# Sink-window attention before two expert layers: folding two pairs' scores in one copy, and moving the attention output ahead of the second pair's maxima

## The chip, the cores and the metric

The program runs on one core of a Trainium2 chip. The metric is the device time of one execution in microseconds (us). The kernel before was run three times: 624.0, 624.75 and 624.91 us, median 624.75. The execution that was profiled took 624.49 us, of which 622.70 are the span that the profiler shows; 1.79 us lie around it.

## What is computed

Inputs are float32: 2 batches, 8 heads, 768 positions, head dimension 64.

```python
scores = scale * np.matmul(q, k.transpose(0, 1, 3, 2))
keep = is_sink | in_window        # pos < 4, or 0 <= rel < 128
scores = np.where(keep, scores, -1000000000.0)
a = np.exp(scores - np.max(scores, axis=-1, keepdims=True))
a = a / (np.sum(a, axis=-1, keepdims=True) + 1e-09)
x = np.matmul(a, v)               # -> 1536 tokens x 512
h = x @ w_in1                     # 512 -> 2048, rational function P(h)/Q(h)
x = g(h) @ w_out1
h = np.maximum(x @ w_in2, 0.0)    # second layer: squared relu
out = (h * h) @ w_out2
```

The expert weights arrive as 64-bit numbers, so each weight tile has to be loaded and narrowed on the chip before TensorE can use it.

## The kernel before, in words

**Two parts.** The first part is the attention, written as steps. A step `u` is one block of 128 query positions with all 8 heads; there are 12 (`NU`), 6 for each batch. The second part is the two expert layers, written as 96 "slots" `k` (48 for each layer). A slot computes one 128-wide slice of the hidden layer for 512 tokens: `g1` (12 matmuls of 512 columns, L620), an elementwise chain on ACT, DVE and POOL (`act_a`, `act_b`, `act_c`), and `g2` (12 matmuls, L699). The last steps of the attention are interleaved with the first slots: `slot(0)` runs `step(12)` in its middle, `slot(1)` runs `step(13)`. The order of instructions on every engine is the order in which the Python program writes them; each engine works its queue strictly in that order.

**One attention step.** Heads come in four pairs `pr`; a half `a` of a step holds two pairs (`k` = 0, 1), and the two heads of a pair are `e` = 0, 1. In step `u` the engines do this, for work of several steps at once:

- TensorE: `scores(u, 0)` and `scores(u, 1)` (L363) multiply the queries with 272 key columns: the block to the left (128 keys and 8 sink columns) and the block's own (128 keys). Only 264 columns are written, and the second pair starts at column 248 (`OFF`) of the same bank. Then `sinks_t(u-2)` (L422) and `trans(u-1)` (L429) transpose earlier results, `pv(u-2)` (L465) multiplies probabilities with values into the one bank called `O`, and `sinks_and_sums(u-2)` (L480, L484) adds the sink keys' values and spreads the reciprocal sums.
- DVE: `fold(u, a)` first copies scores under a mask. A query at place t in its block sees its own block's key j where t >= j, and the left block's key j where t < j, so the two blocks share 128 columns. The copy (`copy_predicated`, L375) is one instruction for a pair, 128 x 2 x 128. Then one custom instruction for each head (L384) adds the mask, scales, writes the negated scores to a tile `ns` (six buffers), and gives their minimum (`nmax`, the negated maximum). `result(u-3)` (L490) multiplies bank `O` with the reciprocals `rb` into `xf`. `sums(u-1)` (L417, L418) adds eps and inverts the sums. At a step's end come steps of the weight narrowing (`w_until`, L241, L247, L253), three to a tile.
- ACT: `expo` (L401) turns `ns` into probabilities and their sums, `trans` copies transposes out (L433), `sinks` and `sinks_t` copy sink columns (L410, L424), `sinks_and_sums` copies `rb` (L486), and `w_fin` rounds a narrowed weight tile (L274).
- POOL: `w_fin` subtracts the rounded weight from the exact one (L275), `parts_of(u-3)` rounds `xf` into `xh` (L497) and takes the remainder `xl` (L498), and `halves(u-1)` splits probabilities into left and own block (L445, L449; L443 in a batch's first block).

**Banks.** PSUM has two score tiles of two banks each (tag `S`), two banks `T`, one `U` and one `O`. `ps_t(tail=True)` takes a bank of a score tile in place of another; the last steps use it. The expert layers' sums (`g2`) also take the two score tiles. With a single bank `O`, the values of step u can be written only after `result(u-1)` has read it:

```python
def pv(m):
    u, a = divmod(m, 2)
    if a == 0:
        ops[u] = ps_t("O")
```

The masks `m_1` and `m_2` for a batch's second block and for later blocks are made once by `setup_rest`, partly on ACT (L140, L147), during steps 0 and 1.

The functions that the change touches, with the line numbers of the profile:

Of the kernel before, what the change touches and what calls it, by code (L numbers as in the profile page):

```python
# [28 lines left out]
NA = 7  # L29
# [9 lines left out]
def kernel(  # L39
# [13 lines left out]
    nc = tc.nc  # L53
# [4 lines left out]
    NU = B * NB  # L58
# [79 lines left out]
    def setup_rest(rel, win, snk, tmp, m_1, m_2, tri):  # L138
        def addm_s(dst, src):
            nc.scalar.activation(out=dst, in_=src, func=ACTF.Identity, scale=BIG, bias=nbig)  # L140

        nc.vector.tensor_scalar(out=tri, in0=rel[:, P:], scalar1=0.0, scalar2=None, op0=ALU.is_lt)
        nc.gpsimd.tensor_tensor(out=tmp, in0=win[:, 0:P], in1=win[:, P:], op=ALU.add)
        nc.gpsimd.tensor_tensor(out=win[:, P:P + SK], in0=snk[:, 0:SK], in1=win[:, 0:SK], op=ALU.subtract)
        yield
        addm_s(m_1[:, SK:], tmp)
        nc.scalar.activation(out=win[:, P:P + SK], in_=win[:, P:P + SK], func=ACTF.Relu)  # L147
        addm_s(m_1[:, 0:SK], win[:, P:P + SK])
        yield
        addm_s(m_2[:, SK:], tmp)  # L150
        addm_s(m_2[:, 0:SK], snk[:, 0:SK])

    def setup_moe():
        nc.scalar.mul(out=na, in_=ab[:, 0:4], mul=-1.0)
# [111 lines left out]
    def w_fin():  # L266
        m = wst["fin"]
        if m not in wx or len(spare) <= keep[0] or int(spare[0][1:]) >= len(wpool):
            return
        wst["fin"] += 1  # L270
        xf = wx.pop(m).bitcast(F32)
        tag = spare.pop(0)
        t = wpool[int(tag[1:])].tile([P, 2, DM], F32R, tag=tag, name="w")
        nc.scalar.copy(out=t[:, 0], in_=xf)  # L274
        nc.gpsimd.tensor_tensor(out=t[:, 1], in0=xf, in1=t[:, 0].bitcast(F32), op=ALU.subtract)  # L275
        W[wtiles[m]] = (t[:, 0], t[:, 1], tag)

# [16 lines left out]
    def attention(ap, extra):  # L294
# [51 lines left out]
        def scores(u, a):  # L346
            i = u % NB
            t = ss[a]
            for k in (1, 0):
                pr, o = 2 * a + k, OFF * k  # L350
                d = [t[:, e, o:] for e in range(2)]
                if i == 0:
                    for e in range(2):
                        s = slice(D * e, D * e + D)
                        nc.tensor.matmul(
                            d[e][:, 0:P], lhsT=ld[u, "q"][s, pr, :], rhs=keys[s, pr, 0, 0:P], start=True, stop=True
                        )
                else:
                    hf = P // 2
                    for g in range(2):  # L360
                        for e in range(2):
                            s, r = slice(D * e, D * e + D), slice(hf * g, hf * g + BS + hf)
                            nc.tensor.matmul(  # L363
                                d[e][hf * g:hf * g + hf, r], lhsT=ld[u, "q"][s, pr, hf * g:hf * g + hf],
                                rhs=keys[s, pr, i - 1:i + 1, :].rearrange("p i n -> p (i n)")[:, r],
                                start=True, stop=True,
                            )

        def fold(u, a):
            i = u % NB  # L370
            mask, co, bw = (m_0, 0, P) if i == 0 else (m_1 if i == 1 else m_2, P, BS)
            pairs = [(k, ss[a][:, :, OFF * k:]) for k in (1, 0)]
            for _, t in pairs:
                if i:
                    nc.vector.copy_predicated(  # L375
                        out=t[:, :, BS:BS + P], mask=tri.unsqueeze(1).to_broadcast([P, 2, P]), data=t[:, :, 0:P]
                    )
            for k, t in pairs:
                n = u * NPR + 2 * a + k
                ns = []  # L380
                for e in range(2):
                    ix = 2 * n + e
                    x = ap.tile([P, 160], F32, name="ns", bufs=6)
                    nc.vector.tensor_tensor_reduce(  # L384
                        out=x[:, 0:bw], in0=t[:, e, co:co + bw], in1=mask, scale=-scale, scalar=3.0e38,
                        op0=ALU.add, op1=ALU.min, accum_out=nmax[:, ix:ix + 1],
                    )
                    ns.append(x)
                kps[n] = ns

        def expo(n):
            u, pr = divmod(n, NPR)
            w = BS if u % NB else P
            if u not in pe_t:
                pe_t[u] = ap.tile([P, NPR, 2, ROW], F32, name="pe", bufs=2)
                rs_t[u] = ap.tile([P, 32], F32, name="rs", bufs=3)[:, 0:H]
            rs, t = rs_t[u], pe_t[u][:, pr]
            ns = kps.pop(n)
            for e in range(2):
                ix = u * H + 2 * pr + e  # L400
                nc.scalar.activation(  # L401
                    out=t[:, e, ROW - w:], in_=ns[e][:, 0:w], func=ACTF.Exp, scale=-1.0,
                    bias=nmax[:, ix:ix + 1], accum_out=rs[:, 2 * pr + e:2 * pr + e + 1],
                )
            pr_t[n] = t

        def sinks(u):
            t = pe_t.pop(u)
            if u % NB:
                nc.scalar.copy(  # L410
                    sr[u % 2][:, 0:HS].rearrange("p (r e s) -> p r e s", r=NPR, e=2),
                    t[:, :, :, ROW - BS:ROW - P],
                )

        def sums(u):
# [10 lines left out]
        def trans(m):  # L426
            d = ps_t(tail=m >= NM - 2)
            for j in range(4):
                nc.tensor.transpose(  # L429
                    d[:, j * P:(j + 1) * P], pr_t[2 * m + j // 2][:, j % 2, ROW - P:], ident  # L430
                )
# [23 lines left out]
        def pv(m):  # L455
            u, a = divmod(m, 2)
            if a == 0:
                ops[u] = ps_t("O")
            pt = pT.pop(m)
            for r in range(2):  # L460
                pr = 2 * a + r
                for j in range(2):
                    for e in range(2):
                        if pt[j] is not None:
                            nc.tensor.matmul(  # L465
                                ops[u][D * e:D * e + D, pr * P:(pr + 1) * P],
                                lhsT=ld[u - 1 + j, "v"][:, 2 * pr + e, :], rhs=pt[j][:, 2 * r + e],
                                start=(pr == 0 and (j == 0 or pt[0] is None)),
                                stop=(pr == NPR - 1 and j == 1), skip_group_check=True,
                            )  # L470
# [58 lines left out]
        def step(u):  # L529
# [6 lines left out]
                        fill(ps_t("T"), DENSE[u][a])  # L536
            if u < NU and u and u % NB == 0:
                sink_keys(u)
            if u < NU:
                fold(u, 0)  # L540
            if 0 <= u - 3:
                result(u - 3)
                parts_of(u - 3)
            if u == 0:
                sink_keys(0)
                rest = setup_rest(*next(masks), m_1, m_2, tri)
                next(rest)
                next(rest)
            if 0 <= u - 1 < NU:
                sinks(u - 1)  # L550
                sums(u - 1)
            if 0 <= u - 2 < NU:
                sinks_t(u - 2)
            if u < NU:
                expo(u * NPR + 1)
            if 0 <= u - 1 < NU:
                trans(2 * u - 2)
                trans(2 * u - 1)
            if u < NU:
                expo(u * NPR)  # L560
                fold(u, 1)
            if u == 1:
                next(rest, None)
            if 0 <= u - 2 < NU:
                pv(2 * u - 4)
# [1 line left out]
            if 0 <= u - 1 < NU:  # L567
                halves(2 * u - 2)
                halves(2 * u - 1)
            if u < NU:  # L570
                expo(u * NPR + 3)
            if 0 <= u - 2 < NU:
                sinks_and_sums(u - 2)
            if u < NU:
                expo(u * NPR + 2)
            if u == 0:
                for t in sr:
                    nc.gpsimd.memset(t, 0.0)
# [6 lines left out]
                load(u + 1, "v")  # L585
            if u < NU and u % NB == 0:
                load_sinks(u // NB)
            if u >= 3:
                for _ in range(4):
                    next(moe, None)  # L590
            if u == NU - 1:
                g1(0)
            if u < NU and u % NB == 1:
# [459 lines left out]
    with tc.tile_pool(name="ap", bufs=1) as ap:  # L1053
        NM = NU * NPR // 2

        def extra(u):
            for _ in range((1, 1, 2)[u] if u < 3 else 0):
                w_load()
            w_until(min(WS * NA, 2 * u))
            if u == NU:  # L1060
                conv["on"] = False
            if u == NU + 1:
                conv["tag"], conv["on"] = "O", True

        attention(ap, extra)
# [49 lines left out]
```

## Time and profile before

| what | value |
|---|---|
| median of 3 runs | 624.75 us (624.0 to 624.91) |
| the profiled execution | 624.49 us, span 622.70 us |
| TensorE busy with matmuls | 599.8 us, 96% of the span |
| DVE, ACT, POOL busy | 428.5, 347.6, 338.6 us |
| share of the chain of waits that ends last | PE 81%, DVE 10%, ACT 6% |
| attention alone (steps 0 to 11) | up to about 78 us |
| last interleaved steps (slots 0 and 1) | about 78 to 98 us |

How to read it: PE is TensorE's matmuls, PEld its weight loads, PEclk the clock that TensorE was granted (1.00 is 2.4 GHz, 0.50 is 1.2 GHz). Busy time of an engine is summed over the whole span, and the two parts of this kernel have different limits, so rows of one stretch say more than the totals. The trace prints a line that holds an instruction and what it waited for; times in it start at the beginning of the span.

### The profile page before, as it was taken

The numbers are of one execution on the slowest core, as the hardware profiler recorded it, in microseconds if no ns is written. First come the engines' busy times: TensorE is split into PE (matmuls) and PEld (weight loads), VectorE is DVE, ScalarE is ACT, GpSimd is POOL, SyncE is SP. The second block draws the span as 40 slices with busy tenths as digits, with TensorE's granted clock in tenths as the row PEclk, the third lists the DMA queues.
The fourth block names the chain that finished last, engine by engine and source line by source line (L and its number), as shares of the span: only waits on it lengthen the run. The fifth ranks groups of instructions, "written<-read, shape, count | busy, mean of one in ns | idle before, by whom it ended". The sixth has DMA issues, their size and how long they took to land.

```text
span 622.7 us, 9780 instructions
## 1 busy us (share of the span) xinstructions
PE 599.8 (96%) x3490; PEld 492.4 (79%) x3490; DVE 428.5 (69%) x875; ACT 347.6 (56%) x734; POOL 338.6 (54%) x309
## 2 busy tenths in 40 slices
PE   7798889999999999999999999999999999999995
PEld 5676778788888878888888888888888888888884
DVE  5998836989989899877768879598594422441421
ACT  5988855888886877877869543243332222222210
POOL 4688765777776767666857575444352222222221
PEclk9999998999999999999999999999999999999999
DMA  8965311422332333111111447557466355500102
GB/s 212 284 184 170 107 35 35 129 83 93 103 103 75 98 98 102 36 67 34 35 34 35 114 157 251 188 175 235 132 207 198 111 194 169 179 25 0 68 0 73
DMA packets 64233, 72.05 MB, mean 116 GB/s; under 512 B 15281, under 2 KB 55217, under 8 KB 64177
## 3 DMA queue, kind: packets, MB, share of 16 engines
q1 hardware_dynamic: 64032, 71.35, 37.3%
q8 instruction: 29, 0.48, 0.3%
q14 instruction: 28, 0.22, 0.1%
q10 hardware_dynamic: 144, 0.00, 0.0%
HBM read 68.20 MB, written 3.15 MB: 115 GB/s over the span
## 4 chain that ended last, share of the span: by engine, by line
PE 81%; DVE 10%; ACT 6%; issue 1%; POOL 0%; DVEq 0%; ACTq 0%
PE s L699 37%; PE T L620 30%; PE U L620 7%; PE O L465 3%; ACT pe L401 2%; PE O L480 1%; DVE ns L384 1%; DVE t L674 1%; DVE U L672 1%; DVE t L670 1%; DVE wx L253 1%; PE s L511 1%; DVE xf L490 1%; ACT U L666 1%; DVE part L728 1%
## 5 line engine op out<-in xcount | busy, mean ns | idle before, releaser
L620 PE MATMUL T<-xh,w 128*128 128x512 f32 x640 | 210.9, 391 | 0.7 <-DVE t L649 0.7
L682 POOL TENSOR_TENSOR gl<-g,gh 128x512 fp32r<-128x512 f32 x48 | 62.2, 1295 | 157.9 <-ACT gh L681 157.8
L620 PEld LDWEIGHTS T<-xh,w 128*128 128x128 f32 x640 | 120.1, 188 | 28.1 <-DVE t L649 2.8
L699 PE MATMUL s<-gh,w 128*128 128x512 f32 x384 | 126.0, 389 | 0.0
L620 PE MATMUL T<-xl,w 128*128 128x512 f32 x320 | 124.6, 389 | 0.0
L699 PE MATMUL s<-w,gh 128*128 128x512 f32 x384 | 118.2, 389 | 0.0
L682 POOL TENSOR_TENSOR gl<-t,gh 128x512 fp32r<-128x512 f32 x48 | 62.2, 1296 | 47.2 <-ACT gh L681 46.3
L275 POOL TENSOR_TENSOR w<-wx,w 128x512 fp32r<-128x512 f32 x64 | 82.8, 1294 | 7.9 <-ACT w L274 7.7
L699 PEld LDWEIGHTS s<-w,gh 128*128 128x128 f32 x384 | 72.1, 188 | 15.1
L699 PEld LDWEIGHTS s<-gh,w 128*128 128x128 f32 x384 | 72.1, 188 | 14.9
L641 POOL TENSOR_TENSOR t<-t,ah 128x512 f32<-128x512 f32 x48 | 62.2, 1297 | 36.6 <-ACT t L638 34.7
L681 ACT CAST gh<-g 128x512 fp32r<-128x512 f32 x48 | 29.9, 623 | 82.1 <-PE s L699 74.8
L699 PE MATMUL s<-gl,w 128*128 128x512 f32 x192 | 74.7, 389 | 0.0
L699 PE MATMUL s<-w,gl 128*128 128x512 f32 x192 | 74.7, 389 | 0.0
L620 PEld LDWEIGHTS T<-xl,w 128*128 128x128 f32 x320 | 60.1, 188 | 12.3
L681 ACT CAST gh<-t 128x512 fp32r<-128x512 f32 x48 | 29.9, 622 | 45.8 <-DVE t L674 40.1
L670 DVE SCALAR_TENSOR_TENSOR t<-t,U 128x512 f32<-128x512 f32 x48 | 33.0, 686 | 30.3 <-ACT U L667 30.2
L655 DVE TENSOR_TENSOR g<-r,T 128x512 f32<-128x512 f32 x32 | 21.8, 683 | 42.5 <-ACT r L645 42.5
L645 ACT ACTIVATE r<-T 128x512 f32<-128x512 f32 x32 | 19.2, 600 | 53.2 <-PE T L620 53.1
L274 ACT CAST w<-wx 128x512 fp32r<-128x512 f32 x64 | 39.3, 616 | 6.4 <-DVE wx L253 6.4
L620 PE MATMUL U<-xh,w 128*128 128x512 f32 x128 | 42.1, 390 | 0.0
L699 PEld LDWEIGHTS s<-gl,w 128*128 128x128 f32 x192 | 36.0, 188 | 7.6
(136 smaller groups left out, 1016.4 us busy)
## 6 DMA issues: line engine op xcount, KB each, us to landing
wr<-in_w_in_dram SPq DMA_DIRECT2D x54, 512.0 KB, 4.1
wr<-in_w_out_dram SPq DMA_DIRECT2D x52, 512.0 KB, 3.8
qr<-in_q_dram SPq DMA_DIRECT2D x12, 256.0 KB, 4.7
keys<-in_k_dram SPq DMA_DIRECT2D x12, 256.0 KB, 4.7
vr<-in_v_dram SPq DMA_DIRECT2D x12, 256.0 KB, 5.2
wr<-in_v_dram SPq DMA_DIRECT2D x6, 512.0 KB, 4.5
out_dram<-part SPq DMA_DIRECT2D x12, 256.0 KB, 2.0
vsc<-in_v_dram SPq DMA_DIRECT2D x2, 16.0 KB
```

The costliest lines, as they stand in the source:

```text
L274: nc.scalar.copy(out=t[:, 0], in_=xf)
L275: nc.gpsimd.tensor_tensor(out=t[:, 1], in0=xf, in1=t[:, 0].bitcast(F32), op=ALU.subtract)
L401: nc.scalar.activation(out=t[:, e, ROW - w:], in_=ns[e][:, 0:w], func=ACTF.Exp, scale=-1.0, bias=nmax[:, ix:ix + 1], accum_out=rs[:, 2 * p ...
L465: nc.tensor.matmul(ops[u][D * e:D * e + D, pr * P:(pr + 1) * P], lhsT=ld[u - 1 + j, "v"][:, 2 * pr + e, :], rhs=pt[j][:, 2 * r + e], start ...
L620: nc.tensor.matmul(h, lhsT=wi[a][:, kk * P:(kk + 1) * P], rhs=(xh, xl)[b][c][:, kk, :], start=(kk == 0 and a + b == 0), stop=(kk == KD - 1 ...
L641: nc.gpsimd.tensor_tensor(out=t, in0=t, in1=ah, op=ALU.mult)
L645: nc.scalar.activation(out=r, in_=h, func=ACTF.Relu)
L655: nc.vector.tensor_tensor(out=g, in0=st.pop(k), in1=h, op=ALU.mult)
L670: nc.vector.scalar_tensor_tensor(out=t, in0=t, scalar=QP, in1=r0, op0=ALU.add, op1=ALU.mult)
L681: nc.scalar.copy(out=gh, in_=g)
L682: nc.gpsimd.tensor_tensor(out=gl, in0=g, in1=gh.bitcast(F32), op=ALU.subtract)
L699: nc.tensor.matmul(acc[L, g, c][m], lhsT=lh, rhs=rh, start=(f == f0 and a + b == 0), stop=(f == f1 and a == 1),)
```

## The change

1. **One masked copy in place of two.** The fold's direction is turned: the own block's scores are copied onto the columns of the left block, where t >= j, and the result stands in columns 0 to 127 with the sinks behind it. In this direction both pairs of a half can be addressed by one access pattern with four dimensions, 128 x 2 x 2 x 128. The mask `tri`, the masks `m_1` and `m_2`, and the readers of the probabilities (`expo`, `sinks`, `trans`) follow the new place. The order of pairs is 0, 1 in place of 1, 0.
2. **xf between two pairs' maxima.** `result(u-3)` and `parts_of(u-3)` are written after the first pair's maxima of `fold(u, 0)`, not after both.
3. **Order on ACT and of the set-up.** `sinks_t(u-2)` comes before `sinks(u-1)`; both of the second half's `expo` come before `sinks_and_sums(u-2)`; the masks `m_1` are made after the first four `expo` instructions; the coefficients of the expert layer are made from step 5 on, one at a time.
4. **Weight tiles in the attention.** The rounding (L274) moves from ACT to POOL while the attention runs, and the narrowing is paced at 7u/4 instructions in place of 2u (21 in all, as before).
5. **The last step's values in a score bank.** `pv` of step 11 takes `ps_t("O", tail=True)`, a bank of a score tile.

```diff
-        nc.vector.tensor_scalar(out=tri, in0=rel[:, P:], scalar1=0.0, scalar2=None, op0=ALU.is_lt)
+        nc.vector.tensor_scalar(out=tri, in0=rel[:, P:], scalar1=0.0, scalar2=None, op0=ALU.is_ge)
...
-        nc.scalar.copy(out=t[:, 0], in_=xf)
+        (nc.gpsimd.tensor_copy if conv["tag"] == "U" else nc.scalar.copy)(out=t[:, 0], in_=xf)
...
-        def fold(u, a):
+        def fold(u, a, between=lambda: None):
             i = u % NB
-            mask, co, bw = (m_0, 0, P) if i == 0 else (m_1 if i == 1 else m_2, P, BS)
-            pairs = [(k, ss[a][:, :, OFF * k:]) for k in (1, 0)]
-            for _, t in pairs:
-                if i:
-                    nc.vector.copy_predicated(
-                        out=t[:, :, BS:BS + P], mask=tri.unsqueeze(1).to_broadcast([P, 2, P]), data=t[:, :, 0:P]
-                    )
-            for k, t in pairs:
+            mask, bw = (m_0, P) if i == 0 else (m_1 if i == 1 else m_2, BS)
+            if i:
+                lo, hi = (
+                    ss[a][:, :, o:o + 2 * OFF].rearrange("p e (k n) -> p e k n", k=2)[:, :, :, x:x + P]
+                    for o, x in ((0, 0), (512 - 2 * OFF, BS + 2 * OFF - 512))
+                )
+                nc.vector.copy_predicated(
+                    out=lo, mask=tri.unsqueeze(1).unsqueeze(1).to_broadcast([P, 2, 2, P]), data=hi
+                )
+            for k in range(2):
+                t = ss[a][:, :, OFF * k:]
...
-                        out=x[:, 0:bw], in0=t[:, e, co:co + bw], in1=mask, scale=-scale, scalar=3.0e38,
+                        out=x[:, 0:bw], in0=t[:, e, 0:bw], in1=mask, scale=-scale, scalar=3.0e38,
...
+                if k == 0:
+                    between()
...
-                ops[u] = ps_t("O")
+                ops[u] = ps_t("O", tail=u == NU - 1)
...
+            fin = (lambda: (result(u - 3), parts_of(u - 3))) if 0 <= u - 3 else (lambda: None)
             if u < NU:
-                fold(u, 0)
-            if 0 <= u - 3:
-                result(u - 3)
-                parts_of(u - 3)
+                fold(u, 0, fin)
+            else:
+                fin()
             if u == 0:
                 sink_keys(0)
                 rest = setup_rest(*next(masks), m_1, m_2, tri)
                 next(rest)
-                next(rest)
+            if 0 <= u - 2 < NU:
+                sinks_t(u - 2)
             if 0 <= u - 1 < NU:
                 sinks(u - 1)
                 sums(u - 1)
-            if 0 <= u - 2 < NU:
-                sinks_t(u - 2)
             if u < NU:
-                expo(u * NPR + 1)
+                expo(u * NPR)
...
             if u < NU:
-                expo(u * NPR)
+                expo(u * NPR + 1)
                 fold(u, 1)
...
             if u < NU:
+                expo(u * NPR + 2)
                 expo(u * NPR + 3)
             if 0 <= u - 2 < NU:
                 sinks_and_sums(u - 2)
-            if u < NU:
-                expo(u * NPR + 2)
...
-            w_until(min(WS * NA, 2 * u))
+            w_until(min(WS * NA, (7 * u) // 4))
```

Where instructions move, the order that each engine is given shows it. DVE in a middle step of the attention, from the first half's copy to the reciprocal. `s` is a score tile, `ns` and `nmax` the negated scores and their minimum, `m_107` the mask, `rs` the sums; each head has two rows, and "..." stands for the next head's. Before:

```order
L375 COPY_PREDICATED s<-tri,s 128x2x128 x2
L384 ISA ns,nmax<-s,m_107 128x136
L384 ISA nmax 128x1
...
L490 TENSOR_TENSOR xf<-O,rb 128x512
L417 TENSOR_TENSOR rs<-rs,eps 128x8
L418 RECIPROCAL sr_155<-rs 128x8
```

With the change:

```order
L377 COPY_PREDICATED s<-tri,s 128x2x2x128
L387 ISA ns,nmax<-s,m_107 128x136
L387 ISA nmax 128x1
...
L495 TENSOR_TENSOR xf<-O,rb 128x512
L387 ISA ns,nmax<-s,m_107 128x136
L387 ISA nmax 128x1
...
L422 TENSOR_TENSOR rs<-rs,eps 128x8
L423 RECIPROCAL sr_155<-rs 128x8
```

Before, four heads' maxima stand ahead of `xf`; now two do, and two stand behind it, ahead of the sums.

ACT in the same stretch, from one `rb` copy to the next (`pe` is the probabilities, two rows to a pair in the trace, `pc` the transposed ones, `st` the transposed sinks). Before:

```order
L486 COPY rb<-T 128x512
L401 ACTIVATE pe,rs<-ns,nmax 128x136 x2
L410 COPY sr_155<-pe 128x64
L424 COPY st<-T 128x128
L401 ACTIVATE pe,rs<-ns,nmax 128x136 x2
L433 COPY pc<-T 128x512 x2
L401 ACTIVATE pe,rs<-ns,nmax 128x136 x4
L486 COPY rb<-T 128x512
```

With the change:

```order
L491 COPY rb<-T 128x512
L429 COPY st<-T 128x128
L415 COPY sr_154<-pe 128x64
L406 ACTIVATE pe,rs<-ns,nmax 128x136 x2
L438 COPY pc<-T 128x512 x2
L406 ACTIVATE pe,rs<-ns,nmax 128x136 x6
L491 COPY rb<-T 128x512
```

The step's last pair of exponentials moved from behind `rb` to ahead of it, and the two small copies changed places.

TensorE at the end of the attention (step 13, in slot 1), with what each row waits for. `sr_155` is the last block's sinks, `ph` its probabilities, `vr` its values. Before:

```order
L422 MATMUL s<-ident,sr_155 128x128 [waits DVE_49,Activation_49]
L465 MATMUL O<-ph,vr 64x128 [waits DVE_49,Pool_49]
...
L480 MATMUL O<-st,vm 64x128 [waits Activation_49]
L484 MATMUL s<-st,bd 64x128 [waits PE_49]
...
L620 MATMUL T<-xh_79,w 128x512
```

With the change:

```order
L427 MATMUL s<-ident,sr_155 128x128 [waits DVE_49,Activation_49]
L470 MATMUL s<-ph,vr 64x128 [waits Activation_49,Pool_49]
...
L485 MATMUL s<-st,vm 64x128 [waits Activation_49]
L489 MATMUL s<-st,bd 64x128
...
L624 MATMUL T<-xh_79,w 128x512 [waits DVE_49]
```

The values' first matmul waited for DVE (`xf` of the block before, which reads bank `O`) and for POOL; now it writes a score bank and waits for ACT (the `rb` copy of the block before, which reads that bank) and for POOL.

## Rows read from the trace of the kernel before

**Rows 1.** The page, part 2: granted clock in 40 slices of 15.57 us.
```profile
PEclk9999998999999999999999999999999999999999
```
**Rows 2.** Busy by stretch: us; PE, PEld, DVE, ACT, POOL (instructions), PEclk, DMA, GB/s.
```profile
8.99:26.75 17.76, 13.37 (x195) 9.69 (x198) 15.34 (x80) 17.61 (x77) 11.78 (x19) 1.00 1.01 296
...
66.44:72.94 6.50, 5.71 (x113) 4.70 (x109) 5.74 (x26) 5.62 (x23) 5.52 (x8) 1.00 0.43 121
...
94.03:97.60 3.57, 3.57 (x36) 3.35 (x39) 0.00 (x0) 0.00 (x0) 1.79 (x2) 0.53 0.00 0
98.56:120.00 21.44, 21.44 (x97) 17.29 (x94) 18.75 (x29) 16.82 (x28) 15.83 (x13) 1.00 0.28 78
```
**Rows 3.** The chain that ended last, step 10: start us, us, what.
```profile
65.70 0.72 PE s L363 x16
66.44 0.44 DVE s L375
...
68.44 0.60 DVE xf L490
...
69.19 1.97 PE O L465 x32
```
**Rows 4.** Timeline, DVE, step 11: start us, us, instruction, count [idle before <-releaser].
```profile
72.94 0.89 DVE L375 COPY_PREDICATED s<-tri,s 128x256 f32<-128x256 int32 x2 [0.45 <-PE s L363]
73.97 0.30 DVE L384 CUSTOM_DVE_ANT_0 ns<-s,m 128x136 f32<-128x136 f32 x1
...
74.86 0.69 DVE L490 TENSOR_TENSOR xf<-O,rb 128x512 f32<-128x512 f32 x1
75.46 0.15 DVE L417 TENSOR_TENSOR rs<-rs,eps 128x8 f32<-128x8 f32 x1
```
**Rows 5.** Timeline, TensorE, steps 3 (first row) and 11.
```profile
24.62 1.97 PE L465 MATMUL O<-ph,vr 128*64 128x128 f32 x32 [0.53 <-DVE rs L417]
...
72.02 1.53 PE L363 MATMUL s<-keys,qr 64*64 64x200 f32 x32
...
73.64 1.18 PE L429 MATMUL T<-ident,pe 128*128 128x128 f32 x8
75.69 1.97 PE L465 MATMUL O<-ph,vr 128*64 128x128 f32 x32 [0.87 <-DVE rs L417]
```
**Rows 6.** Groups of POOL, 0 to 100 us: count, busy us, mean ns, idle before.
```profile
L497 POOL CAST xh<-xf 128x512 fp32r<-128x512 f32 x11 | 6.7, 613 | 8.4 <-DVE rs L417 4.9 <-DVE xf L490 3.1
```
**Rows 7.** Timeline, ACT, step 0.
```profile
8.99 0.40 ACT L140 ACTIVATE m<-su,nbig 128x128 f32<-128x128 f32 x1 [6.90 <-POOL su L143]
...
9.73 0.39 ACT L401 ACTIVATE pe<-ns,nmax 128x128 f32<-128x128 f32 x1
```
**Rows 8.** Timeline, DVE, step 0.
```profile
7.17 0.29 DVE L384 CUSTOM_DVE_ANT_0 ns<-s,m 128x128 f32<-128x128 f32 x1 [0.58 <-PE s L355]
```
**Rows 9.** Timeline, TensorE, step 13 (the end of the attention).
```profile
91.21 0.27 PE L422 MATMUL s<-ident,sr 128*128 128x128 f32 x1
94.03 3.57 PE L465 MATMUL O<-ph,vr 128*64 128x128 f32 x32 [2.54 <-DVE xf L490]
```
**Rows 10.** Timeline, ACT, steps 12 and 13.
```profile
88.52 0.59 ACT L486 COPY rb<-s 128x512 f32<-128x512 f32 x1 [2.35 <-PE s L484]
...
98.70 0.59 ACT L486 COPY rb<-s 128x512 f32<-128x512 f32 x1 [6.30 <-PE s L484]
```
**Rows 11.** Timeline, POOL, step 12: the last block's last half.
```profile
88.84 0.64 POOL L449 TENSOR_SCALAR_AFFINE_SELECT ph<-pc 128x512 f32<-128x512 f32 x1
```
**Rows 12.** Timeline, DVE, step 13: the last xf.
```profile
99.39 0.69 DVE L490 TENSOR_TENSOR xf<-O,rb 128x512 f32<-128x512 f32 x1 [5.51 <-ACT rb L486]
```
**Rows 13.** Timeline, DVE, step 6.
```profile
43.11 1.08 DVE L417 TENSOR_TENSOR rs<-rs,eps 128x8 f32<-128x8 f32 x1
```
**Rows 14.** Timeline, POOL, step 6.
```profile
42.89 1.28 POOL L275 TENSOR_TENSOR w<-wx,w 128x512 fp32r<-128x512 f32 x1 [0.78 <-ACT w L274]
44.10 0.35 POOL L342 COPY keys<-keys 128x192 f32<-128x192 f32 x1
```

More of the change, by code (lines that the diff above doesn't have):

```diff
@@ L145, in setup_rest @@
         yield
-        addm_s(m_1[:, SK:], tmp)
+        addm_s(m_1[:, 0:P], tmp)
         nc.scalar.activation(out=win[:, P:P + SK], in_=win[:, P:P + SK], func=ACTF.Relu)
-        addm_s(m_1[:, 0:SK], win[:, P:P + SK])
+        addm_s(m_1[:, P:], win[:, P:P + SK])
         yield
-        addm_s(m_2[:, SK:], tmp)
-        addm_s(m_2[:, 0:SK], snk[:, 0:SK])
+        addm_s(m_2[:, 0:P], tmp)
+        addm_s(m_2[:, P:], snk[:, 0:SK])
     def setup_moe():
@@ L348, in scores @@
             t = ss[a]
-            for k in (1, 0):
+            for k in range(2):
                 pr, o = 2 * a + k, OFF * k
@@ L367, in scores @@
                             )
-        def fold(u, a):
+        def fold(u, a, between=lambda: None):
             i = u % NB
-            mask, co, bw = (m_0, 0, P) if i == 0 else (m_1 if i == 1 else m_2, P, BS)
-            pairs = [(k, ss[a][:, :, OFF * k:]) for k in (1, 0)]
-            for _, t in pairs:
-                if i:
-                    nc.vector.copy_predicated(
-                        out=t[:, :, BS:BS + P], mask=tri.unsqueeze(1).to_broadcast([P, 2, P]), data=t[:, :, 0:P]
-                    )
-            for k, t in pairs:
+            mask, bw = (m_0, P) if i == 0 else (m_1 if i == 1 else m_2, BS)
[7 more added lines that the diff above has]
+                )
+            for k in range(2):
+                t = ss[a][:, :, OFF * k:]
                 n = u * NPR + 2 * a + k
@@ L401, in expo @@
                 nc.scalar.activation(
-                    out=t[:, e, ROW - w:], in_=ns[e][:, 0:w], func=ACTF.Exp, scale=-1.0,
+                    out=t[:, e, 0:w], in_=ns[e][:, 0:w], func=ACTF.Exp, scale=-1.0,
                     bias=nmax[:, ix:ix + 1], accum_out=rs[:, 2 * pr + e:2 * pr + e + 1],
@@ L411, in sinks @@
                     sr[u % 2][:, 0:HS].rearrange("p (r e s) -> p r e s", r=NPR, e=2),
-                    t[:, :, :, ROW - BS:ROW - P],
+                    t[:, :, :, P:BS],
                 )
@@ L429, in trans @@
                 nc.tensor.transpose(
-                    d[:, j * P:(j + 1) * P], pr_t[2 * m + j // 2][:, j % 2, ROW - P:], ident
+                    d[:, j * P:(j + 1) * P], pr_t[2 * m + j // 2][:, j % 2, 0:P], ident
                 )
@@ L547, in step @@
                 next(rest)
-                next(rest)
+            if 0 <= u - 1 < NU:
+                pass
+            if 0 <= u - 2 < NU:
+                sinks_t(u - 2)
             if 0 <= u - 1 < NU:
@@ L559, in step @@
             if u < NU:
-                expo(u * NPR)
+                expo(u * NPR + 1)
                 fold(u, 1)
-            if u == 1:
+            if u < 2:
                 next(rest, None)
@@ L587, in step @@
                 load_sinks(u // NB)
-            if u >= 3:
-                for _ in range(4):
-                    next(moe, None)
+            if u >= 5:
+                next(moe, None)
             if u == NU - 1:
```

## The prediction, made before the change was run

> **What bounds the kernel now.** I read the page first: matmuls fill 96% of the span, and the granted clock dips once, in the seventh of 40 slices [rows 1]. So the question is where TensorE isn't yet the limit. The table by stretch answers it [rows 2]: from 98.56 us on TensorE is busy in 21.44 of 21.44 us, and the 96% leave little idle time anywhere else. Whatever comes before 98.56 us shifts everything behind it; whatever lies after it and isn't a matmul is hidden. The change touches only the part before.
>
> In a middle step of the attention (66.44 to 72.94) no engine is full: TensorE 5.71, DVE 5.74, ACT 5.62, POOL 5.52 of 6.50 us [rows 2]. The chain of waits shows why a step takes 6.50 all the same [rows 3]: scores, copies, maxima, `xf`, values, scores, on TensorE and DVE in turn. With one bank `O`, the values wait for `xf`, and the next scores stand behind the values in TensorE's queue. The timelines give the pieces [rows 3 to 5]: values to next scores 69.19 to 72.02, 2.83; scores to copies 72.02 to 72.94, 0.92; copies to first maximum 1.03; four maxima 73.97 to 74.86, 0.89; `xf` to values 74.86 to 75.69, 0.83. Together 6.50.
>
> **The steps.** The change shortens two pieces of this loop. First, the copy. Two instructions of 256 columns took 0.89 from start to end, one alone 0.44 [rows 3, 4]; `xf`, 512 columns out of PSUM, took 0.69 [rows 4]. So 256 columns more cost about 0.25, and I take 0.69 for the copy of 512: 0.20 saved. The trace has no masked copy of 512; the bounds are 0.44 (width costs nothing, 0.45 saved) and 0.89 (nothing saved), and I take the value at `xf` because its width and its PSUM source are the same. The Trainium skill ("VectorE: DVE Perf Modes", the section on the TRN2 errata) gives 120 cycles of fixed cost to an instruction that reads PSUM. By that one instruction fewer saves an estimated 0.125, and the sum would come out 0.6 us higher; the trace's 0.44 for 256 columns is above the page's 0.39, so I go by the rows.
>
> Second, two of four maxima leave the path to `xf`: 0.45. The loop becomes 6.50 - 0.20 - 0.45 = 5.85 us.
>
> What is late next? TensorE's own queue needs, from scores to transposes 1.62 (72.02 to 73.64), transposes 1.18, and 2.83 from values to next scores [rows 3, 5]: 5.63. DVE's 5.74 lose two savings of 0.2 and a quarter of a narrowing instruction (0.17, at the 0.69 of 512 columns), and keep 0.31 of hand-overs (6.50 - 5.74, less the 0.45 it waits for scores [rows 4]): about 5.5. ACT loses the weight rounding and stays near 5.1. POOL gains 0.61 for it [rows 6] in a step with a weight tile, 6.1, which is over 5.85; but only seven tiles come, the other steps need 1.3 + 0.6 less, and its probabilities are wanted a whole step later. The moved sums also wait for POOL: `rs` now comes 1.05 after the start of `xf`, when POOL rounds the new `xf`, and I allow 0.3 for that (below). DVE then stands at 5.8. With three queues at 5.6 to 5.85, I take 5.9: **0.6 saved a step**. From the values of step 3 at 24.62 to those of step 11 at 75.69 there are 8 intervals (51.07 us) [rows 5]: 8 x 0.6 = **4.8 us**. Bounds: 3.6 (only the maxima, 0.45) to 7.0 (TensorE's 5.63).
>
> The moved `expo` puts `rb` behind one more pair of exponentials (0.8), and `xf` waits for `rb` with two maxima queued behind it. In the new loop `rb` is done about 1.1 after the scores start, and `xf` is due 0.92 + 0.83 + 0.45 = 2.2 after: no wait. Nothing on SP moves past a transfer that a step needs within its next 5.9 us; I cost the DMA order at nothing.
>
> **The start.** ACT's first exponential began at 9.73, behind three mask instructions that waited for POOL and began at 8.99 [rows 7]; the first maximum began at 7.17 [rows 8], so the scores were ready by about 7.6. From 8.99 to 26.75 ACT was busy 17.61 of 17.76 us [rows 2]: here ACT is the limit. Now four exponentials (1.55) fill the wait, then the masks (0.74): the fifth starts at 9.85, not 11.3, **1.4** sooner. By the first `xf` DVE sheds more: five copies x 0.2, one narrowing 0.69, two maxima 0.45, in all 2.1, but ACT and DVE share the wait. Bounds 1.4 to 3.2; I take **2.4**.
>
> **The end.** The last block's values could start at 91.48, behind the transpose at 91.21 [rows 9]; they waited 2.54 us for `xf` of the block before, and then ran in 3.57 us at a granted clock of 0.53, the 1.2 GHz level [rows 2, 9], where the same 32 took 1.97 at 2.4 GHz [rows 5]. In a score bank they wait for `rb` of the block before (88.52 + 0.59 [rows 10]) and for POOL's last half (88.84 + 0.64 [rows 11]): both are done. So 2.54 goes, the clock doesn't fall, and 1.60 goes with it: **4.1 us**. What is late next: the sums of the first expert slot need the bank back, so the last `xf` (99.39 [rows 12]) must end before them; they start 12 matmuls after 98.56, at 101.2. Both move up together, since `xf` follows the last `rb` (98.70 [rows 10]) and that follows the values: slack 1.1 as before. Bounds 0 (the wait turns up there) to 4.1.
>
> **The sum.** 4.8 + 2.4 + 4.1 = 11.3. The profiled execution took 624.49 (span 622.70 and 1.79 around it), 0.26 under the median of 624.75: 613.2 on its own scale, 613.4 on the median's; I say **613.3 us**. The ends of this case: 7.0 + 3.2 + 4.1 gives 610.2; 3.6 + 1.4 + 4.1 gives 615.4.
>
> **Rivals.** *The wait at the end only moves* to the first expert sums, through the last `xf` or POOL's remainder ahead of it: 4.1 less, 617.4. For it: POOL's queue there has a rounding more. Against: POOL idled in that stretch (1.79 of 3.57 us busy [rows 2]). *DVE or POOL takes over the steps* at about 6.2: 8 x 0.3 + 1.4 + 4.1, 616.6. For it: the queues are within 0.3 us of each other. *The copy over four dimensions costs double per column*, about 1.25: DVE needs 6.9 a step, 0.4 more than now; 8 x 0.4 - 1.4 - 4.1 = -2.3, 622.2. Nothing in the rows speaks for it; a pattern of three dimensions ran at the normal rate.
>
> *Slower: the sums stuck behind POOL.* `rs`, a DVE addition of 8 columns, takes 0.15 [rows 4], but 1.08 in step 6, where POOL's subtraction ran, and it ended at 44.19, as that ended at 44.17 [rows 13, 14]. It stood right behind `xf`, before POOL could start on it; now it stands two maxima later, inside POOL's row of rounding (0.61 [rows 6]), remainder (1.28) and four halves (0.64 each [rows 11]). If POOL kept going through that row, `rs` and the second half's copies would wait 4.0 us a step: 9.5 in place of 6.5, and 24 - 6.5 = 17.5 slower, 642. It decides from a wait of 2.0 on; behind the remainder alone (1.6) the whole would come to 623. Against it: in step 6 POOL's next copy had already begun at 44.10, and `rs` still got in [rows 14]. The Trainium skill ("SBUF — State Buffer", Who interferes with whom) says that GpSimd and a DVE instruction with two SBUF inputs exclude each other for a whole instruction. By that rule the change does cost something, the 0.3 above; the trace agrees with it, and no run shows who wins between two queued POOL instructions but this one row.
>
> **How the numbers follow.** Forecast 0.65; wait only moves 0.12; DVE or POOL takes over 0.12; costly copy 0.04; sums behind the remainder 0.03, behind the row 0.04. The first three, 0.89, lie between 610 and 617.6, which is my range; with some spill at its ends it holds 8 in 10. A measurement of this kernel tells 0.2% (1.25 us) from no change. Faster 0.92: the first four cases, less 0.01 for a copy dearer still. Same 0.04: the sums behind the remainder, which come out near that bound, and that 0.01. Slower 0.04: the sums behind the row.
>
> **What would show it.** Right: about 5.9 us between the values of middle steps; one copy near 0.69; first exponential near 7.6; the last values right behind their transpose, 1.97 long, with no dip of the clock; TensorE full from about 87 us. Wrong: `rs` over 1 us in most steps, TensorE idle before the first expert sums, or a copy of 1 us and more.

## The result, and the profile after

The changed kernel takes 613.13 us (median of 4 runs, 612.95 to 613.95), the kernel before 624.74 (4 runs beside it, 624.0 to 624.91). The ratio is 0.9819, interval 0.9802 to 0.9836. The forecast was 613.3, its range 610.0 to 617.6. The profiled execution took 613.21 us, with a span of 611.4 in place of 622.70.

| stretch, us | before | after | less | predicted |
|---|---|---|---|---|
| start to the values of step 3 | 24.62 | 23.17 | 1.45 | 2.4 |
| values of step 3 to those of step 11 | 51.07 | 46.07 | 5.00 | 4.8 |
| values of step 11 to the third slot's first `g1` matmul | 22.87 | 18.65 | 4.22 | 4.1 |
| from there to the end of the span | 524.14 | 523.51 | 0.63 | 0 |

The sum is 11.30, the difference of the spans. That the total meets the forecast within 0.2 us is partly luck: the start fell short by 0.95, and three smaller surpluses, 0.63 of them after the attention, made up for it. The borders are rows of TensorE: 24.62 and 75.69 before [rows 5], 98.56 before [rows 2], and after:

```profile
23.17 1.97 PE L470 MATMUL O<-ph,vr 128*64 128x128 f32 x32 [0.38 <-DVE xf L495]
69.24 1.97 PE L470 MATMUL O<-ph,vr 128*64 128x128 f32 x32 [0.24 <-DVE xf L495]
84.75 0.27 PE L427 MATMUL s<-ident,sr 128*128 128x128 f32 x1
84.95 1.97 PE L470 MATMUL s<-ph,vr 128*64 128x128 f32 x32
87.89 0.50 PE L624 MATMUL T<-xh,w 128*128 128x512 f32 x1
90.74 0.40 PE L703 MATMUL s<-gh,w 128*128 128x512 f32 x1
```

The last values (84.95) follow their transpose at once, with no wait, and take 1.97 us where they had waited 2.54 and taken 3.57 [rows 9]. The row of granted clock on the page has lost its dip [rows 1]; the 8 at its end lies at the program's end.

```profile
PEclk9999999999999999999999999999999999999998
```

Busy time by stretch in the kernel after (columns as in [rows 2]): the start, a middle step, and the first expert slots.

```profile
7.97:23.17 15.20, 12.28 (x163) 8.86 (x161) 13.13 (x69) 14.71 (x67) 10.76 (x19) 1.00 0.98 268
...
61.26:67.12 5.86, 5.62 (x113) 4.70 (x109) 5.42 (x23) 5.30 (x23) 5.70 (x8) 1.00 0.51 134
...
87.00:108.44 21.44, 21.44 (x121) 17.37 (x118) 18.47 (x30) 16.82 (x28) 17.53 (x15) 1.00 0.25 75
```

TensorE is full from 87.00 us on, so no wait has moved to the expert sums (`g2`, 90.74). A middle step takes 5.86 us in place of 6.50, and its busiest engine is now POOL, at 5.70. The chain of waits in the same step, as before with one copy and two maxima ahead of `xf` (start us, us, what):

```profile
60.51 0.72 PE s L363 x16
61.26 0.71 DVE s L377
...
62.40 0.21 DVE ns L387
62.62 0.61 DVE xf L495
63.24 0.14 issue
63.37 1.97 PE O L470 x32
```

The same on DVE's timeline, with the first maximum of the program, the first narrowing instruction (its wait for a weight's transfer is taken up in the start, below), a later one, one `rs`, and the last `xf`:

```profile
7.64 0.29 DVE L387 CUSTOM_DVE_ANT_0 ns<-s,m 128x128 f32<-128x128 f32 x1 [0.73 <-PE s L355]
...
15.19 0.70 DVE L241 TENSOR_SCALAR U<-wr 128x512 int32<-128x512 int32 x1 [0.66 <-DMA wr<-in_w_in_dram]
...
49.18 0.69 DVE L253 SCALAR_TENSOR_TENSOR wx<-wr,U 128x512 int32<-128x512 int32 x1
...
57.72 0.35 DVE L422 TENSOR_TENSOR rs<-rs,eps 128x8 f32<-128x8 f32 x1
...
61.26 0.70 DVE L377 COPY_PREDICATED s<-tri,s 128x512 f32<-128x512 int32 x1 [0.77 <-PE s L363]
...
62.54 0.69 DVE L495 TENSOR_TENSOR xf<-O,rb 128x512 f32<-128x512 f32 x1
...
88.71 0.69 DVE L495 TENSOR_TENSOR xf<-s,rb 128x512 f32<-128x512 f32 x1 [1.29 <-ACT rb L491]
```

The masked copy of 512 columns took 0.70, against 0.89 for two of 256 [rows 4]. `rs` took 0.35, against 0.15 [rows 4], and POOL's timeline shows why: the rounding of the new `xf` began at 57.43 and ended at 58.04, and `rs` ended at 58.07.

```profile
49.11 1.28 POOL L335 TENSOR_TENSOR vm<-bd,vsc 64x512 f32<-64x512 f32 x1
...
57.43 0.61 POOL L502 CAST xh<-xf 128x512 fp32r<-128x512 f32 x1 [0.86 <-DVE xf L495]
58.13 1.28 POOL L503 TENSOR_TENSOR xl<-xf,xh 128x512 fp32r<-128x512 f32 x1
```

ACT after: the first exponential now runs ahead of the masks (9.73 and 8.99 before [rows 7]), and the last `rb` follows the last values.

```profile
7.97 0.40 ACT L406 ACTIVATE pe<-ns,nmax 128x128 f32<-128x128 f32 x1 [5.88 <-DVE nmax L387]
...
9.53 0.39 ACT L140 ACTIVATE m<-su,nbig 128x128 f32<-128x128 f32 x1
...
88.02 0.59 ACT L491 COPY rb<-s 128x512 f32<-128x512 f32 x1 [2.09 <-PE s L489]
```

### The profile page after: what moved, and what is told of

Read it like the earlier page. It is cut to its first block, busy times and chain, and to the rows that moved or that the text cites. A ratio compares the mean times of both kernels' runs of the same rounds, so it can differ in the third digit from the quotient of the medians.

```text
span 611.4 us, 9769 instructions
## 1 busy us (share of the span) xinstructions
PE 597.7 (98%) x3490; PEld 491.4 (80%) x3490; DVE 424.8 (69%) x855; ACT 342.9 (56%) x727; POOL 342.7 (56%) x316
## 4 chain that ended last, share of the span: by engine, by line
PE 71%; DVE 15%; ACT 10%; issue 2%; DMA 1%; DVEq 0%; ACTq 0%
PE s L703 32%; PE T L624 25%; PE U L624 7%; DVE t L678 3%; PE O L470 2%; DVE U L676 2%; ACT U L670 2%; ACT U L671 2%; ACT gh L685 2%; ACT w L274 2%; ACT pe L406 2%; DVE t L674 1%; DVE ns L387 1%; DVE O L241 1%; DVE wx L253 1%
## 5 line engine op out<-in xcount | busy, mean ns | idle before, releaser
L406 ACT ACTIVATE pe<-ns,nmax 128x136 f32<-128x136 f32 (+1 forms) x96 | 38.0, 400 | 7.2 <-DVE nmax L387 7.0
```

The costliest lines, as they stand in the source:

```text
L406: nc.scalar.activation(out=t[:, e, 0:w], in_=ns[e][:, 0:w], func=ACTF.Exp, scale=-1.0, bias=nmax[:, ix:ix + 1], accum_out=rs[:, 2 * pr + e ...
```

## The experiments

Each edit is made to the changed kernel, but for one that is made to the kernel before. They ran in four groups, each with the kernel before beside it, at medians of 624.15 to 624.42. A full step is one away from the second batch's first block, which has no copy and shortens the steps around it. The filler matmuls ahead of the first scores (L516, on a tile of zeros), which no edit touches, took 5.01 to 6.20 us from profile to profile, so stretches are compared by intervals between values.

**The score bank undone.**

```diff
-                ops[u] = ps_t("O", tail=u == NU - 1)
+                ops[u] = ps_t("O")
```

> The changed kernel with the last step's values back in bank O; nothing else differs. Theory (the wait for xf of the block before, 2.54 us, and the fall of the clock behind it, 1.6 us, were removed by the score bank): both come back, the values of step 13 run at about half clock again, 3.6 us long, and the time rises from 613.1 by about 4.2 to 617.3 us. Rival (the end gained only because the steps before it got shorter, and another wait ends at the same place): 613.1 us, no dip of the clock.

617.12 us (616.76 to 618.41), ratio 0.9894 [0.9872, 0.9916]. TensorE's timeline shows the old end, the wait of 2.54 and values of 3.55 us at a granted clock of 0.53 (2.54, 3.57 and 0.53 in the kernel before [rows 2, 9]):

```profile
86.83 3.55 PE L470 MATMUL O<-ph,vr 128*64 128x128 f32 x32 [2.54 <-DVE xf L495]
91.37 0.50 PE L624 MATMUL T<-xh,w 128*128 128x512 f32 x1
```

From the values of step 11 (68.46) to the third slot it is 22.91, 4.26 more than after. The time is 4.0 longer. Full steps stay at 5.86.

**The score bank alone, in the kernel before.** The same line, edited the other way.

> The kernel before, with one edit alone: the last block's values take a bank of a score tile. If the end is a part of its own, the values of step 11 to the third run of the first expert matmuls take 18.65 us in place of 22.87, the last values run in 1.97 us, steps stay at 6.5, and the time is 624.6 - 4.2 = 620.4. Rival: the other edits pay in part for the end (the bank order needs them, or the wait at the end is 2.54 us only because steps are what they are): the end takes over 20 us and the time is 622 or more.

620.08 (619.82 to 620.88), ratio 0.9933 [0.9915, 0.9951]. Values of step 11 at 75.63, third slot at 94.28: 18.65, as in the changed kernel, with steps of 6.5. The end is a part of its own.

```profile
91.35 1.97 PE L465 MATMUL s<-ph,vr 128*64 128x128 f32 x32
94.28 0.50 PE L620 MATMUL T<-xh,w 128*128 128x512 f32 x1
```

**`xf` behind both pairs' maxima.**

```diff
-                if k == 0:
-                    between()
+            between()
```

> The changed kernel with xf behind both pairs' maxima of the first half, as before; the single copy stays. Theory (the loop scores, copy, maxima, xf, values sets the step): a step becomes 5.86 + 0.45 = 6.3 us, 8 steps and the first xf give about +4.0: 617.1 us. Rival (the step is set by DVE's own queue, which holds the same work in either order): 613.1 to 613.6 us with steps of 5.9.

615.96 (615.6 to 616.02), ratio 0.9868 [0.9849, 0.9887]. Full steps take 6.30, 0.44 more than 5.86. The time is 1.1 below the theory's 617.1, which counted 0.45 in each of eight intervals and in the start: from the values of step 3 to those of step 11 it is 48.84 in place of 46.07, 2.77 more, as two of the three intervals around the second batch's first block grew by 0.18 and not at all, and the start didn't grow. DVE, then TensorE in that kernel:

```profile
63.20 0.70 DVE L377 COPY_PREDICATED s<-tri,s 128x512 f32<-128x512 int32 x1 [1.39 <-PE s L363]
64.93 0.68 DVE L494 TENSOR_TENSOR xf<-O,rb 128x512 f32<-128x512 f32 x1
65.53 0.15 DVE L421 TENSOR_TENSOR rs<-rs,eps 128x8 f32<-128x8 f32 x1
```

```profile
59.46 1.97 PE L469 MATMUL O<-ph,vr 128*64 128x128 f32 x32 [0.86 <-DVE rs L421]
65.76 1.97 PE L469 MATMUL O<-ph,vr 128*64 128x128 f32 x32 [0.67 <-DVE rs L421]
```

DVE idles 1.39 us for the scores, so its queue isn't what sets this step: the two maxima are, on the path to `xf`. And `rs`, directly behind `xf` again, takes 0.15.

**Two copies in place of one.**

```diff
-                nc.vector.copy_predicated(
-                    out=lo, mask=tri.unsqueeze(1).unsqueeze(1).to_broadcast([P, 2, 2, P]), data=hi
-                )
+                for k in range(2):
+                    t = ss[a][:, :, OFF * k:]
+                    nc.vector.copy_predicated(
+                        out=t[:, :, 0:P], mask=tri.unsqueeze(1).to_broadcast([P, 2, P]), data=t[:, :, BS:BS + P]
+                    )
```

> The changed kernel with one masked copy for each pair (two of 256 columns) in place of one for two pairs; direction and everything else stay. Theory: 0.20 us more in the loop of each of 8 steps and about 0.2 at the start, +1.8: 614.9 us. Rival A (DVE's queue sets the step, and both halves' copies count): +0.4 a step, 616.5 us. Rival B (copies are covered by waits for TensorE): 613.1 us.

616.08 (615.56 to 616.94), ratio 0.9876 [0.9856, 0.9896], between the theory (614.9) and its rival A (616.5), and nearer the rival. Full steps take 6.06 to 6.27: 0.20 more where the loop alone counts, up to 0.41 where DVE's queue counts too (the second half's copies cost it another 0.20). On DVE:

```profile
62.98 0.89 DVE L375 COPY_PREDICATED s<-tri,s 128x256 f32<-128x256 int32 x2 [0.57 <-PE s L363]
...
65.50 0.47 DVE L420 TENSOR_TENSOR rs<-rs,eps 128x8 f32<-128x8 f32 x1
```

**The weights' rounding back on ACT.**

```diff
-        (nc.gpsimd.tensor_copy if conv["tag"] == "U" else nc.scalar.copy)(out=t[:, 0], in_=xf)
+        nc.scalar.copy(out=t[:, 0], in_=xf)
```

> The changed kernel with the rounding of weight tiles on ACT again. Theory (ACT has some 0.7 us free in a step of 5.86 and its copy rb is wanted 1 us later than it is done): 613.1 to 613.5 us. Rival (ACT is near its limit, and 0.5 us in each of five steps lands on the path): 615.6 us. Rival on the other side (POOL's extra instruction costs DVE waits of its own): a little below 613.1 us.

614.08 (613.21 to 614.83), ratio 0.9836 [0.9814, 0.9859], above the theory's 613.5 and far below the rival's 615.6. Full steps stay at 5.86; two shorter ones take 5.95 and 5.93 in place of 5.81 and 5.65, with `rs` up to 0.59. The interval holds the changed kernel's ratio, so this part of the change is not told from nothing.

**The narrowing paced at 2u again.**

```diff
-            w_until(min(WS * NA, (7 * u) // 4))
+            w_until(min(WS * NA, 2 * u))
```

> The changed kernel with the narrowing of weights paced at 2u instructions again in place of 7u/4. Theory (DVE's queue is within 0.1 to 0.3 us of the loop, and two narrowing instructions in every step put it over): two or three steps grow by 0.1 to 0.3 us, 613.3 to 613.8 us. Rival (DVE has room): 613.1 us. Rival on the other side (tiles that are ready sooner help the first expert slots): 612.5 us.

613.84 (613.7 to 615.15), ratio 0.9838 [0.9824, 0.9851], which overlaps the changed kernel's interval: not told from nothing either. Two steps grew as the theory said (5.78 in place of 5.65, 5.95 in place of 5.87), and the time is at the upper end of its range.

**The masks ahead of the exponentials, as before.**

```diff
-            if 0 <= u - 1 < NU:
-                pass
+                next(rest)
...
-            if u < 2:
+            if u == 1:
                 next(rest, None)
```

> The changed kernel with the masks m_1 made ahead of the first exponentials again, as before. Theory (ACT is the limit from its first exponential to about 22 us): the first exponential starts near 10 us, some 1.4 us pass on to the first values, 614.5 us. Rival (DVE or TensorE is the limit at the start): 613.1 to 613.4 us.

614.35 (613.41 to 614.52), ratio 0.9835 [0.982, 0.985]. In that kernel DVE's first maximum, ACT's first mask and first exponential, and TensorE's values of step 3:

```profile
7.81 0.29 DVE L387 CUSTOM_DVE_ANT_0 ns<-s,m 128x128 f32<-128x128 f32 x1 [1.30 <-PE s L355]
```

```profile
9.63 0.40 ACT L140 ACTIVATE m<-su,nbig 128x128 f32<-128x128 f32 x1 [7.54 <-POOL su L143]
...
10.37 0.38 ACT L406 ACTIVATE pe<-ns,nmax 128x128 f32<-128x128 f32 x1
```

```profile
24.10 1.09 PE L470 MATMUL O<-ph,vr 128*64 128x128 f32 x16
```

(The view ends inside the last row; 24.10 is the start of those values.) From first maximum to first exponential 2.56 in place of 0.33, 2.2 more; from first maximum to the values of step 3, 16.29 in place of 15.53, 0.8 more. But the changed kernel's 15.53 holds a wait of 0.66 for the first weight tile (`wr`, L241), and here DVE reached that instruction later, at 15.55, and didn't wait: without the wait the difference is 1.4. By the times alone the two kernels aren't told apart.

**The step's last exponentials behind `rb`, as before.** `expo(u * NPR + 3)` is written behind `sinks_and_sums(u - 2)`.

> The changed kernel with the step's last pair of exponentials behind rb again. Theory (rb is done about 1 us before xf wants it, so its place is free; the last exponentials come later and hold ns buffers and the transposes): 613.1 to 613.8 us. Rival (xf waits for rb in the changed kernel): below 612.5 us.

612.66 (612.47 to 612.87), ratio 0.9813 [0.98, 0.9827]. The time lies between the theory's 613.1 and the rival's 612.5, and the intervals of the ratios overlap. Middle steps stay at 5.86, so there `rb` isn't awaited. The interval between the values of steps 2 and 3 is 5.43 in place of 5.92, but DVE's wait for the first weight tile is 0.19 in place of 0.66, and that is 0.47 of the 0.49:

```profile
14.37 0.70 DVE L241 TENSOR_SCALAR U<-wr 128x512 int32<-128x512 int32 x1 [0.19 <-DMA wr<-in_w_in_dram]
```

**The sums right behind `xf`**, ahead of POOL's work on it (`sums(u - 1)` is written between `result(u - 3)` and `parts_of(u - 3)`, from step 3 on).

> The changed kernel with the two small instructions on the sums right behind xf (from step 3 on), ahead of the second pair's maxima, where they stood before. Theory (they wait for POOL's rounding of the new xf, which cannot have begun there): the addition takes 0.16 in place of 0.35 us in nearly all steps. DVE gains 0.2 a step, but where the loop over TensorE sets the step nothing follows: 612.5 to 613.2 us. Rival (the addition's length has nothing to do with POOL): it stays near 0.35 us and the time at 613.1.

614.43 (612.93 to 614.59), ratio 0.9837 [0.9824, 0.9851]. No gain, and above the theory's 613.2. Only half of the theory on `rs` held: it takes 0.15 to 0.16 in some steps and 0.33 to 0.64 in the others, where it meets POOL's work on a weight tile. DVE's first narrowing instruction, which didn't wait for its weight tile here, then DVE and POOL in one of those steps:

```profile
14.41 0.69 DVE L241 TENSOR_SCALAR U<-wr 128x512 int32<-128x512 int32 x1
...
50.97 0.64 DVE L422 TENSOR_TENSOR rs<-rs,eps 128x8 f32<-128x8 f32 x1
```

```profile
50.31 1.28 POOL L275 TENSOR_TENSOR w<-wx,w 128x512 fp32r<-128x512 f32 x1
```

**`xf` right behind the copy**, ahead of both pairs' maxima.

```diff
+            between()
             for k in range(2):
...
-                if k == 0:
-                    between()
```

> The changed kernel with xf right behind the copy, ahead of both pairs' maxima. Theory (the loop through copy, maxima, xf and values sets the step): the loop loses another pair of maxima, 5.86 - 0.44 = 5.42; TensorE's own queue (5.63, from scores to transposes to values to scores) is then the limit, so steps of about 5.65 and 613.1 - 8 x 0.2 = 611.5. Rival A: DVE's queue of work and hand-overs is full before that, at 5.75 to 5.85: 612.3 to 613.1. Rival B: the exponentials start 0.62 later in each step, and ACT or the transposes behind them are late: steps of 5.9 and over, 613.5 or more.

613.88 (613.67 to 614.02), ratio 0.9829 [0.9815, 0.9843]: nothing gained, where the theory had 611.5 and rival B 613.5 or more. The steps fall into two kinds: 5.65 to 5.77, and three of 6.21 to 6.33. Each of the three stands behind an `rs` of 1.26 to 1.28 us. One of each kind on TensorE, and DVE and POOL in the long one:

```profile
52.13 1.09 PE L469 MATMUL O<-ph,vr 128*64 128x128 f32 x16
57.85 1.97 PE L469 MATMUL O<-ph,vr 128*64 128x128 f32 x32
64.06 1.97 PE L469 MATMUL O<-ph,vr 128*64 128x128 f32 x32
```

```profile
56.88 0.69 DVE L494 TENSOR_TENSOR xf<-O,rb 128x512 f32<-128x512 f32 x1
58.36 1.27 DVE L421 TENSOR_TENSOR rs<-rs,eps 128x8 f32<-128x8 f32 x1
```

```profile
57.64 0.61 POOL L501 CAST xh<-xf 128x512 fp32r<-128x512 f32 x1 [0.41 <-DVE xf L494]
58.33 1.27 POOL L502 TENSOR_TENSOR xl<-xf,xh 128x512 fp32r<-128x512 f32 x1
59.56 0.63 POOL L449 TENSOR_SCALAR_AFFINE_SELECT ph<-pc 128x512 f32<-128x512 f32 x1
```

With four maxima between `xf` and the sums, `rs` comes 1.48 us after `xf` starts, just after POOL began the remainder, and ends at 59.63, as that ends at 59.60. Rival B has a part: in four steps `xf` waited 0.24 to 0.95 us for `rb`. But two of those waits fall in short steps, and the first long step has none, so they don't explain that two kinds of step exist; nor does a DVE that is full in every step.

**The last two edits together.** `xf` right behind the copy, the last exponentials behind `rb`.

> The changed kernel with xf right behind the copy and with the step's last pair of exponentials behind rb again, as in the kernel before. With xf wanted 0.44 sooner, rb wanted sooner too: if rb is what is late in the run with xf first alone, this one is faster by what xf waits for rb there; if not, it adds the same 0.4 us as that edit did alone (612.66 against 613.1), so about 611.1 by the theory of a step of 5.65, 612 to 612.7 by the rival of a full DVE.

612.42 (612.34 to 613.59), ratio 0.9814 [0.9798, 0.983]. From the values of step 3 to those of step 11 it is 46.29, against 47.33 with `xf` first alone, and `xf` no longer waits for `rb`. The time lies in the range of the rival of a full DVE (612 to 612.7), not at the theory's 611.1, so it takes one more run to tell these apart. Behind an `rs` of 1.25 to 1.28 steps of 5.91 to 6.41 remain.

**And the sums between the two pairs' maxima**, so that `rs` comes as soon after `xf` as in the changed kernel.

```diff
                 n = u * NPR + 2 * a + k
+                if k == 1:
+                    mid()
...
-                fold(u, 0, fin)
+                fold(u, 0, fin, (lambda: sums(u - 1)) if u >= 3 else (lambda: None))
```

> The last kernel (xf right behind the copy, last pair of exponentials behind rb) with the sums between the two pairs' maxima, 1.06 us after xf starts, as in the changed kernel, in place of 1.48 after, behind both pairs. Theory (in the two runs with xf first, the steps of 6.2 to 6.4 are those in which rs met POOL's remainder and took 1.25 to 1.28): rs meets the rounding alone and takes about 0.35, no step is over 5.8, and the four long intervals (6.41, 6.24, 5.91, 5.78 against 5.55) give back some 2 us: 610.5. Rival A: the long steps have another cause (a DVE queue too full for the weight narrowing), steps of 6.2 stay while rs is 0.35: 612 or more. Rival B: rs now waits for other POOL instructions (a weight's rounding or subtraction) or for the exponentials behind rb, which end later: rs over 0.6 in several steps, 611.5 to 612.5.

611.33 (611.12 to 612.64, 5 runs), ratio 0.9799 [0.9781, 0.9817]: the fastest kernel here. All full steps take 5.55 to 5.77, and from the values of step 3 to those of step 11 it is 44.98. The theory's mechanism holds: with `rs` away from the remainder the long steps are gone. The time is 0.8 above its 610.5. Here too rival B has a part: where `rs` meets POOL's weight subtraction it takes up to 0.96, and the step behind that one takes 5.70. In a step of 5.55 TensorE has no idle time left (by stretch):

```profile
61.39:66.94 5.55, 5.55 (x106) 4.67 (x105) 5.45 (x24) 4.82 (x21) 4.88 (x8) 1.00 0.36 99
```

Against the changed kernel that is 1.8 us by the medians and 1.9 by the spans (609.5 against 611.4), and no run of the one reaches into the runs of the other; the two were timed on different occasions, and the intervals of their ratios overlap.

## Why the prediction was right, point by point

- **The steps.** Predicted 4.8, measured 5.00. The loop came out at 5.86 where 6.50 - 0.20 - 0.45 gave 5.85. That the total agrees too is partly luck. The prediction took 0.6 for all eight intervals. Four saved 0.63 to 0.64, but the three around the second batch's first block saved 0.59, 0.64 and 0.34, and the first saved 0.88, from 6.74, where `rs` had taken 0.90 in the kernel before. Both terms were shown apart: full steps took 0.44 more with `xf` behind four maxima, and 0.20 more at least with two copies.
- **The copy.** Taken at 0.69, it took 0.67 to 0.70. The saving of 0.20 came from rows; the Trainium skill's fixed cost ("VectorE: DVE Perf Modes", the section on the TRN2 errata), which the page states for PSUM to SBUF, would have made it an estimated 0.125, and the trace of this copy, PSUM to PSUM, does not agree with that.
- **The step that was too careful.** "With three queues at 5.6 to 5.85, I take 5.9." No queue took over: 5.86 is the loop. The last run shows where the next limit lies: 5.55, TensorE's own queue, estimated at 5.63.
- **The sums and POOL.** The 0.3 allowed for `rs` is 0.2 where it meets the rounding (0.35 less 0.15); over the steps of the changed kernel it took 0.16 to 0.45. The rival in which `rs` is stuck behind POOL's row didn't come about, nor the one behind the remainder. Its mechanism is real, though: with `xf` 0.44 earlier `rs` met the remainder and took 1.27. It never waited for more than the POOL instruction that was running.
- **The start.** Predicted 2.4, 1.45 in the profiled run. What the sum lacked is a wait: DVE, now earlier, came to the first narrowing instruction before its weight tile had landed, stood 0.66 us (15.19 in the kernel after), and the next masked copy stands behind it in DVE's queue. The kernel before reached that instruction at 15.11 and didn't wait. From the first maximum to the values of step 3 four runs took 15.53, 15.29 (the score bank undone), 15.04 (the last exponentials behind `rb`) and 14.85 (the sums right behind `xf`). Up to that instruction they are alike. Their waits there were 0.66, 0.43, 0.19 and none, and without them all four give 14.85 to 14.87, 2.6 less than the 17.45 before. Another 0.47 is no work of the change: the first maximum began at 7.64, not 7.17 [rows 8], because the filler matmuls ahead of the scores took 5.82 in place of 5.36. So 2.6 - 0.66 - 0.47 = 1.5. The prediction costed the DMA order at nothing because no transfer moved; it didn't ask which engine would come sooner to a transfer. Its 1.4 for the masks stands: undoing that cost 16.29 - 14.86 = 1.4 where nothing waited for the tile. Its upper bound of 3.2 isn't worked out; the two parts that it names, 1.4 and 2.1, add up to 3.5.
- **`rb` behind one more pair of exponentials** was costed at nothing. The runs agree, in a middle step and in the start: what the run with `rb` early gained there is the shorter wait for the weight tile.
- **The end.** Predicted 4.1, measured 4.22, and shown from both sides: undone 4.0 us longer, alone 4.07 to 4.66 faster than the kernel before (medians 624.15 and 624.74 of its runs). The expert sums didn't wait: the last `xf` ended at 89.40, they began at 90.74.
- **The rest.** 0.63 less after the attention wasn't predicted. That stretch took 523.6 to 523.9 in all twelve experiments, whatever their edit, the one on the kernel before among them, so no part of the change has been shown to cause it.

Undone one at a time, the copy (2.95), `xf` (2.83), the bank (3.99) and the masks (1.22) sum to 11.0 of the 11.6 us. These are differences of medians from different occasions, and the masks' isn't clear of noise, so the sum is a rough one. The exchange of ACT's two small copies and the later coefficients were not tried alone.

## What to carry to other kernels

Follow the chain of waits in one middle step, add up its pieces, and take out of the sum only what stands between the wait and its releaser; then compare with each engine's own queue, as that is the next limit. Where a small instruction shares a resource with another engine, its place in the queue decides its cost: ask which instruction of the other engine will be running when it comes. And where a change lets an engine run ahead, look for what it will reach too soon: a transfer that always landed in time may now be awaited, and everything behind it in that queue with it.

## What the runs showed of the hardware

A DVE addition of 8 columns with both inputs in SBUF waited out one POOL instruction: it ended 0.02 to 0.03 us after a rounding (58.07 and 58.04), a remainder (59.63 and 59.60) or a weight's subtraction (51.61 and 51.59), and POOL's next instruction, which followed at once, did not keep it waiting. The Trainium skill ("SBUF — State Buffer", Who interferes with whom) has it that a DVE instruction with two SBUF inputs contends with a GpSimd instruction that reads SBUF, for ports under an exclusive lock; the traces agree, and add that the waiting DVE instruction gets in at the hand-over. A narrowing instruction, whose second input lies in PSUM, ran 0.69 us inside POOL's 1.28 (49.18 and 49.11 in the kernel after) and was no longer than elsewhere.

A masked copy over four dimensions cost no more per column than `xf`: 0.67 to 0.70 for 512. And 14 filler matmuls at the very start, alike in all kernels, took 5.01 to 6.20 us, which moves the whole program; what sets that was left open.
